# Raw expert weights in four buffers that rotate in program order, one size register, held products flushed earlier, and padding products

## The chip, the cores and the metric

The program runs on one core of one Trainium2 chip, in one launch. The metric is device time in microseconds (us). The kernel before took 292.46 us (median of three runs, 291.24 to 293.19). One further execution was profiled; the rows below are from it.

TensorE (PE) multiplies, with a weight load (PEld) ahead of each product; VectorE (DVE), ScalarE (ACT) and GpSimd (POOL) work element by element; SyncE (SP) issues transfers, and POOL issues the indirect ones (gathers and scatters).

## The reference

Linear attention over four batches, eight heads, 768 positions and 48 channels feeds a gated mixture of eight experts:

```python
for t in range(S):
    cur = einsum('bhd,bhe->bhde', u * k[t], v[t])
    y[t] = einsum('bhd,bhde->bhe', r[t], state + cur)
    state = w[t][..., None] * state + einsum('bhd,bhe->bhde', k[t], v[t])
x = y.transpose(0, 2, 1, 3).reshape(3072, 384)
out = x.copy()
xc = x[x @ w_skip > 0]
logits = xc @ w_gate                 # (tokens, 8)
e_idx = argmax(logits)               # one expert per token
gate = softmax(logits)[e_idx]
for e in range(8):
    m = e_idx == e
    out[those tokens] += gate[m] * (relu(xc[m] @ w1[e]) @ w2[e])   # 384 -> 1024 -> 384
```

Data are float32 throughout, and which expert gets how many tokens is known only at run time.

## The kernel before, in words

**Attention.** The 3072 rows are 24 chunks of 128 positions. A loop over "slots" s runs from -2 to 24, and each slot works on several chunks at once. POOL makes the cumulative products of chunk s+2 (p L370, rk L372, wrk L379, kq L400); DVE makes two scans (L384, L402), rp (L407), two masks (asb L436) and a bonus (psY L448) per slot; PE makes psu L458, the outputs L484 and L490, the scores L420 from rp and kq, the sums L444 and the row products L505. psu, psY, psA0 and psA1 are PSUM banks. SP stores each finished chunk (L520).

**The router.** Tokens are routed in three groups of chunks, (0, 12), (12, 6) and (18, 6). The router is a generator whose steps are dripped into the slots after the group's last chunk, a fixed number per slot (`drip`, `pace`); it makes one-hot rows (`hots`, on DVE or, by `by_act`, ACT) and sums on PE. Pieces for PE that it appends to `held` (the ranks at L562 to L568, the places at L617, into the psu bank) are run by `flush()`, which stands at the end of each slot. A DVE step behind such a piece comes in program order as soon as it has been flushed.

**Expert 0, early.** Slots 22 to 24 and the stretch behind also carry expert 0's first 128 tokens: their indices id0, the gather xg0 (L656), transposes (L671), layer 1 (L151, into psH) and layer 2 (L701, into psO). Then the router's last group gives idr; POOL issues the gather xg1 of expert 0's second 128 tokens (L525) and those of expert 1; the sizes of the experts (`few`, eight digits 0, 1 or 2) go into eight registers of PE (L842); xg1 is transposed (L671) and expert 0's layer 1 follows for them (`second`, L919). For each of four banks it branches: 96 columns where size 0 is positive, 128 else.

**Experts 1 to 7.** Each does layer 1 (L934 to L936) and layer 2 (L958, L964) on up to 256 tokens, with weights split into a high and a low part: the raw weights arrive by SP (`load_weights`, two halves of 1.5 MB for each expert, three transfers each), ACT casts the high part (L131), and POOL or DVE subtract to get the low part (L135). Raw halves lie in buffers r00, r10, r01 and r11. Three more kinds of work fill in: scatters of results (L912), gathers of expert e+2's tokens (L525), and a check of the decay products (wp, L866 to L881).

**What sets the order.** Attention and all engines but SP in the expert phase follow program order. SP's transfers of the expert phase are put in order by a scheduler.

## Time and profile before

| | |
|---|---|
| median of three runs | 292.46 us |
| the profiled execution, whole | 291.64 us |
| its span in the trace | 289.8 us |
| busy share of the span: PE, DVE, POOL, ACT | 91%, 76%, 68%, 52% |
| moved | 65.08 MB, 225 GB/s |

The span is the part of the execution that the trace covers; 1.84 us lie around it. The page lists, for 40 slices of the span, how busy each engine was and which clock PE was granted; the chain of waits follows the work that ended last back to its start; the timeline lists instructions in order of start, with the idle time ahead of each and what ended it.

### The profile page before, as it was taken

How to read it: one execution, taken by the hardware profiler on the slowest of the kernel's cores; microseconds unless marked ns; L12 is line 12 of the kernel's file. 1: busy time of each engine (PE TensorE's matmuls, PEld its weight loads, DVE VectorE, ACT ScalarE, POOL GpSimd, SP SyncE). 2: the span in 40 equal slices, each digit the busy share in tenths (PEclk: the TensorE clock that was granted, in tenths of full speed). 3: DMA queues.
4: the chain of work that ended last, by engine and by line, in shares of the span. 5: the costliest groups of instructions: out<-in, count | busy, mean ns of one | idle time of the engine just before them, and what ended most of it. 6: DMA issues, size and time to landing. Idle time of an engine off the chain costs nothing.

```text
span 289.8 us, 9303 instructions
## 1 busy us (share of the span) xinstructions
PE 263.3 (91%) x3695; PEld 232.8 (80%) x3695; DVE 220.3 (76%) x431; ACT 150.1 (52%) x365; POOL 196.4 (68%) x176
## 2 busy tenths in 40 slices
PE   7769999989899798888986999999999999999990
PEld 2458888878687686677876999997999999998880
DVE  6988999889999879996282355888785788779931
ACT  5134434443467525424530546668694957769710
POOL 6889999999876857769962323783865548545711
PEclk9999999999999899999998699999999999999998
DMA  6999999999978798856097986117678781998001
GB/s 170 241 232 274 276 279 275 270 280 250 276 225 235 220 283 212 263 172 231 29 317 257 349 287 233 55 54 271 250 259 274 253 318 47 323 349 309 29 11 46
DMA packets 27699, 65.08 MB, mean 225 GB/s; under 512 B 4172, under 2 KB 15408, under 8 KB 27638
## 3 DMA queue, kind: packets, MB, share of 16 engines
q1 hardware_dynamic: 25318, 58.39, 66.5%
q0 software_dynamic: 2048, 5.48, 5.5%
q8 instruction: 39, 0.64, 1.0%
q10 hardware_dynamic: 272, 0.39, 0.5%
q14 instruction: 22, 0.18, 0.2%
HBM read 57.20 MB, written 7.86 MB: 225 GB/s over the span
## 4 chain that ended last, share of the span: by engine, by line
PE 69%; DVE 11%; DMA 9%; POOL 4%; issue 3%; ACT 2%; SPq 1%; DVEq 0%; POOLq 0%; ACTq 0%
PE psO L958 17%; PE psH L948 7%; PE psY L484 5%; PE psA L420 5%; PE psH L934 4%; PE psH L936 4%; PE psH L935 4%; DMA wrk<-wrk 4%; PE psX L505 4%; PE psH L151 4%; PE psY L490 4%; PE psY L444 3%; DVE asb L436 3%; PE psO L964 3%; DMA xg<-out,idr 2%
## 5 line engine op out<-in xcount | busy, mean ns | idle before, releaser
L135 POOL TENSOR_TENSOR w2l<-r,w2h 128x512 fp32r<-128x512 f32 x25 | 33.0, 1340 | 15.2 <-ACT w2h L131 14.9
L912 POOL DMA_INDIRECT out<-fin,ids x16 | 20.4, 1275 | 33.5 <-DMA xg<-out,idr 9.5
L400 POOL TENSOR_TENSOR kq<-wrk,q 128x512 f32<-128x512 f32 x24 | 26.9, 1120 | 16.1 <-DVE q L384 10.7
L379 POOL TENSOR_TENSOR wrk<-wrk 128x512 f32<-128x512 f32 x24 | 36.2, 1508 | 1.7
L436 DVE TENSOR_TENSOR asb<-psA,c_sb 128x512 f32<-128x512 f32 x48 | 30.8, 683 | 6.2 <-PE psA L420 5.8
L1001 DVE SCALAR_TENSOR_TENSOR hl<-psH,hh 128x512 fp32r<-128x512 f32 (+1 forms) x32 | 20.8, 654 | 18.5 <-ACT hh L1000 18.5
L958 PE MATMUL psO<-w2h,hh 128*128 128x384 f32 x96 | 32.8, 342 | 0.0
L135 DVE TENSOR_TENSOR w1l<-r,w1h 128x512 fp32r<-128x512 f32 x30 | 32.6, 1102 | 0.0
L958 PE MATMUL psO<-w2l,hh 128*128 128x384 f32 x96 | 32.1, 335 | 0.0
L496 ACT COPY xT<-psY 128x512 f32<-128x512 f32 x24 | 14.1, 586 | 34.0 <-PE psY L490 28.8
L484 PE MATMUL psY<-asb,vN 128*64 128x128 f32 (+1 forms) x384 | 25.8, 276 | 4.9 <-DVE psY L448 4.7
L525 POOL DMA_INDIRECT xg<-out,idr x15 | 17.2, 1145 | 18.6 <-DMA out<-fin,ids 14.0
L131 ACT CAST w2h<-r 128x512 fp32r<-128x512 f32 x48 | 27.5, 648 | 3.4 <-DMA r<-w 3.4
L372 POOL TENSOR_TENSOR rk<-wrk 128x512 f32<-128x512 f32 x22 | 28.1, 1277 | 0.0
L420 PE MATMUL psA<-rp,kq 64*64 64x128 f32 (+1 forms) x768 | 26.5, 256 | 1.1 <-DVE rp L407 0.6
L934 PE MATMUL psH<-xTh,w1h 128*128 128x224 f32 (+1 forms) x96 | 26.8, 279 | 0.0
L936 PE MATMUL psH<-xTh,w1l 128*128 128x224 f32 (+1 forms) x96 | 26.5, 276 | 0.0
L935 PE MATMUL psH<-xTl,w1h 128*128 128x224 f32 (+1 forms) x96 | 26.5, 276 | 0.0
L484 PEld LDWEIGHTS psY<-asb,vN 128*64 128x64 f32 (+1 forms) x384 | 20.4, 130 | 6.5 <-DVE psY L448 6.1
L131 ACT CAST w1h<-r 128x512 fp32r<-128x512 f32 x42 | 25.6, 633 | 0.0
L1000 ACT ACTIVATE hh<-psH 128x512 fp32r<-128x512 f32 (+1 forms) x32 | 18.2, 570 | 12.4 <-PE psH L936 6.7
L420 PEld LDWEIGHTS psA<-rp,kq 64*64 64x64 f32 x768 | 22.6, 136 | 2.3 <-POOL kq L400 0.9
(169 smaller groups left out, 696.3 us busy)
## 6 DMA issues: line engine op xcount, KB each, us to landing
r<-w SPq DMA_DIRECT2D x48, 512.0 KB, 5.3
wrk<-wrk SPq DMA_DIRECT2D x23, 577.9 KB, 6.1
wp<-wrk SPq DMA_DIRECT2D x9, 516.0 KB, 8.0
vN<-vN SPq DMA_DIRECT2D x12, 384.0 KB, 4.8
out<-x SPq DMA_DIRECT2D x24, 192.0 KB, 4.0
vt<-wrk SPq DMA_DIRECT2D x24, 96.0 KB, 5.0
vt<-wrk SPq DMA_DIRECT2D x48, 48.0 KB, 4.4
out<-fin,ids POOLq DMA_INDIRECT x16, 4.4
```

The source lines that it names most:

```text
L131: nc.scalar.copy(hi, raw)
L135: eng.tensor_tensor(lo, raw, hi.bitcast(F32), op=ALU.subtract)
L372: (nc.gpsimd if i > 1 else nc.vector).tensor_tensor(rk.rearrange("p a j -> p (a j)"), t[:, R_OFF:K_OFF], t[:, K_OFF:V_OFF], op=ALU.mult)
L379: nc.gpsimd.tensor_tensor(rk1, rk1, two(1, 1, CW), op=ALU.mult)
L400: nc.gpsimd.tensor_tensor(pairs(kq), pairs(wk["k"]), twice(wk["q"][:, :, 1:HW]), op=ALU.mult)
L420: nc.tensor.matmul(psa[g][j:j + HP, a, j:], wk["kq"][rows, a, j:j + HP], wk["rp"][rows, a, j:], start=True, stop=True)
L436: nc.vector.tensor_tensor(s, psa[g], tri.rearrange("p (o j) -> p o j", o=1).to_broadcast([P, NP, P]), op=ALU.mult)
L484: nc.tensor.matmul(quarter(0, a, g, w), head(i, 2 * a + g, w), wk["asb"][g][:, a], start=False, stop=(c == 0), skip_group_check=True)
L934: nc.tensor.matmul(ps, w1h[:, o:o + P], xh, start=(kc == 0), stop=False)
L935: nc.tensor.matmul(ps, w1h[:, o:o + P], xl, start=False, stop=False)
L936: nc.tensor.matmul(ps, w1l[:, o:o + P], xh, start=False, stop=(kc == KC - 1))
L958: nc.tensor.matmul(pso, h[j, fc][k], w[:, fc * DM:(fc + 1) * DM], start=(i == 0), stop=(i == len(todo) - 1))
```

## The change

Six things change.

1. **Raw buffers.** From expert 2 on, the halves rotate over r11, r01, r00, r10 in this order, each half in one transfer of 1.5 MB where there were three of 512 KB. SP joins the engines in program order. The second half of expert 1 is loaded in slot 23, ahead of the store of chunk 23. Expert 2's halves are made to wait for ACT's copy of the transposed xg1.
2. **Gathers.** xg4 and xg5 (expert 2's tokens) are issued with xg1 to xg3, ahead of the scatters.
3. **Sizes.** DVE multiplies the eight digits by powers of four and sums them; PE loads one register, and each branch tests two bits of it.
4. **Expert 0's second 128 tokens.** The branch goes: always 128 columns. Four memsets on DVE that went with it go too.
5. **Held pieces.** Up to slot 17 `flush()` comes after the scores of the next chunk and ahead of the drip that ends the slot. In the first group ACT makes eight one-hot rows, not six, and DVE four, not six. Two low parts of expert 0's second-layer weights move from slots 21 and 22 to slots 13 and 14 on POOL. In slot 23 the last drip comes after the transposes.
6. **Padding.** In slot 0 PE gets ten products of zeros, 5, 2 and 3 of them, at three places.

```diff
 W_AT = {7: ((0, 1),), 11: ((0, 1),), 15: ((0, 1),), 17: ((0, 0),), 19: ((0, 0),), 20: ((0, 0), (1, 0)),
-        21: ((1, 0), (1, 0))}
+        21: ((1, 0), (1, 0)), 23: ((1, 1), (1, 1), (1, 1))}
 CAST_AT = {9: ((0, 6),), 10: ((0, 7),), 13: ((0, 8),), 14: ((0, 9),), 18: ((0, 10),), 19: ((0, 11),),
            22: ((1, 0), (1, 1)), 23: ((1, 2), (1, 3)), 24: ((1, 4), (1, 5))}
-LOW_AT = {21: ((0, 6), (0, 7), (0, 8)), 22: ((0, 9), (0, 10), (0, 11)), 23: ((1, 0), (1, 1), (1, 2)),
-          24: ((1, 3), (1, 4), (1, 5))}
+LOW_AT = {13: ((0, 6),), 14: ((0, 7),), 21: ((0, 8), (0, 9)), 22: ((0, 10), (0, 11)),
+          23: ((1, 0), (1, 1), (1, 2)), 24: ((1, 3), (1, 4), (1, 5))}
 KEYS_AT = {-2: (), -1: (0,), 0: (1,), 1: (2, 3)}
...
                                                mybir.DependencyReason.DATA),
-                          reason="shared port")
+                          reason="behind the gather")
     WN = ("w1h", "w1l", "w2h", "w2l")
...
     def load_weights(e, q):
-        pool, tag = (wset1[0], "r11") if q and e % 2 and e > 1 else (wset0, ("r00", "r10", "r01")[
-            2 * (e % 2) if not q else 1])
+        pool, tag = (wset0, "r" + ("00", "10", "01", "10")[2 * (e % 2) + q]) if e < 2 else (
+            (wset1[0], "r11"), (wset0, "r01"), (wset0, "r00"), (wset0, "r10"))[2 * (e % 2) + q]
         wr = pool.tile([P, KC * DF], F32, tag=tag, name=f"{tag}_{e}{q}")
         raws[e, q] = wr
-        for i in range(3):
-            o = i * 1024
-            nc.sync.dma_start(wr[:, o:o + 1024],
-                              w12[e, :, q * KC * DF + o:q * KC * DF + o + 1024])
-            yield 1
+        m = 3 if e < 2 else 1
+        w = KC * DF // m
+        for i in range(m):
+            o = i * w
+            yield nc.sync.dma_start(wr[:, o:o + w],
+                                    w12[e, :, q * KC * DF + o:q * KC * DF + o + w])
...
         ohs = keep.tile([P, 1, E], BF16, name="ohs")
+        digit = keep.tile([P, E], F32, name="digit")
         short = keep.tile([1, 1, 1], BF16, name="short")
...
             nc.vector.memset(ohs, 0.0)
+            for e in range(E):
+                nc.gpsimd.memset(digit[FEW - P:FEW - P + 1, e:e + 1], float(4 ** e))
             nc.vector.memset(ex_sb, 1e-9)
...
                                       op=ALU.is_equal)
-            by_act = () if last else range(0, m, 2) if m == MG else (0,)
+            by_act = () if last else [c for c in range(m) if c % 3] if m == MG else (0,)
             order = [c for c in range(m) if c in by_act] + [c for c in range(m) if c not in by_act]
...
                 nc.tensor.transpose(ps[:, kc], xg[j][:, kc * P:(kc + 1) * P], ident)
-            nc.scalar.copy(xT0[j], ps)
-
-        hfs = []
+            copied.append(nc.scalar.copy(xT0[j], ps))
+
+        hfs, copied = [], []
...
             nc.vector.scalar_tensor_tensor(fin0, pso, gate0, xg[0], op0=ALU.mult, op1=ALU.add)
+
+        def pad(k):
+            for _ in range(k):
+                nc.tensor.matmul(psr, warm[:, :P], warm, start=False, stop=True,
+                                 skip_group_check=True)
...
                         later.append(early())
+            if s == 0:
+                pad(5)
             if on(s):
                 update(s)
+            if s == 0:
+                pad(2)
             slot[0], spot[0] = s, 1
...
                 outputs(s)
+            if s == 0:
+                pad(3)
             if s == -1:
...
                     quadratic(s + 1)
+                if s < LATE:
+                    flush()
                 spot[0] = 3
                 drip(2 * pace[0])
-            elif s == n - 1:
-                drip(1)
             for i in KEYS_AT.get(s, (s + 2,)):
...
                     keys(i)
+            if s == n - 1:
+                drip(1)
             if s == n - 2:
...
                 rows_out(s)
-            flush()
+            if s >= LATE:
+                flush()
             for i in LOW_AT.get(s, ()):
...
         idf = keep.tile([P, 2, E], F32, name="idf")
-        few = keep.tile([P, E], I32, name="few")
+        few = keep.tile([P, E], F32, name="few")
+        size_i = keep.tile([P, 1], I32, name="size_i")
         ids = keep.tile([P, 2, E], U32, name="ids")
...
                 done[0] += 1
-        drain(load_weights(1, 1))
         early_low(1)
...
             gather(s, None)
-        step = few[FEW - P:FEW - P + 1]
+        step, sizes = few[FEW - P:FEW - P + 1], size_i[FEW - P:FEW - P + 1]
         nc.vector.tensor_scalar(step, gates[FEW - P:FEW - P + 1, 1], 0.0, None, op0=ALU.is_equal)
...
                                        op0=ALU.is_equal, op1=ALU.add)
+        nc.vector.tensor_tensor(step, step, digit[FEW - P:FEW - P + 1], op=ALU.mult)
+        with nc.allow_low_precision(reason="whole numbers"):
+            nc.vector.tensor_reduce(sizes, step, axis=AX, op=ALU.add)
         for k in range(done[0], 6 * FC - 4):
             next(todo)
-        regs = nc.values_load_multi_w_load_instructions(
-            step, engines=[mybir.EngineType.PE], min_val=0, max_val=2)[1]
-        size = dict(enumerate(regs))
+        size = nc.values_load_multi_w_load_instructions(
+            sizes, engines=[mybir.EngineType.PE], min_val=0, max_val=2 * (4 ** E - 1) // 3)[1][0]
         early_tokens(1)
...
                                      accum_out=viol[:, i:i + 1])
-                if e == E - 1:
-                    fetch_w()
...
-        def second(bank, q, m):
-            for i in range(2):
-                for kc in range(KC):
-                    hidden(bank[:, 0, i * P:i * P + m], xT0[1][:, :, :m], 2 * q + i, kc)
-
         def layer1(e, q, bank):
...
             def larger():
-                with tc.If(size[e] > 0) as cmp:
+                with tc.If((size & 4 ** e) > 0) as cmp:
                     rounded(MID)
...
                 return
-            with tc.If(size[e] > 1) as cmp:
+            with tc.If((size & 2 * 4 ** e) > 0) as cmp:
                 for ps, kc, o in tiles:
...
             h, hf = {}, {}
-            if e == 0:
-                for bank in psh:
-                    nc.vector.memset(
-                        bank[:, 0].rearrange("p (i j) -> p i j", i=2)[:, :, MID - P:], 0.0)
             for q in range(FC // 2):
...
                 if e == 0:
-                    with tc.If(size[0] > 0) as cmp:
-                        second(bank, q, MID - P)
-                    with cmp.Else():
-                        second(bank, q, P)
+                    for i in range(2):
+                        for kc in range(KC):
+                            hidden(bank[:, 0, i * P:(i + 1) * P], xT0[1], 2 * q + i, kc)
                 else:
...
                 flag_sums()
-            if e < E - 2:
-                drain(load_weights(e + 2, 0))
+            if e == 0 or 1 < e < E - 2:
+                drain(load_weights(max(e + 2, 3), 0))
             if e + 1 < E:
...
                 scatter(0, fin0)
-            if e + 2 < E:
+            if 0 < e < E - 2:
                 for s in (2 * e + 4, 2 * e + 5):
...
                         check_w(e, 1 if e < E - 1 else E)
+                        if W_FROM - 1 <= e < E - 1:
+                            fetch_w()
+                            fetch_w()
                 pso = psos[j]
...
                     psx = ps1.tile([P, 512], F32, tag="psT", name=f"psX3{e}", bufs=2)[:, :DM]
-                    with tc.If(size[e] > 1) as cmp:
+                    with tc.If((size & 2 * 4 ** e) > 0) as cmp:
                         layer2_few(e, hf, pso, psx)
...
             more(12, left=0)
-            if e + 2 < E:
-                drain(load_weights(e + 2, 1))
-            if W_FROM - 1 <= e < E - 1:
-                fetch_w()
-                fetch_w()
+            if e == 0 or 1 < e < E - 2:
+                drain(load_weights(max(e + 2, 3), 1))
         with tc.manual_schedule(engines={nc.tensor.engine, nc.scalar.engine, nc.vector.engine,
-                                         nc.gpsimd.engine}):
+                                         nc.gpsimd.engine, nc.sync.engine}):
+            for s in (4, 5):
+                gather(s, moe)
+            for q in range(2):
+                for load in load_weights(2, q):
+                    beside(load, copied[1])
             nc.gpsimd.memset(zero, 0.0)
```

How the instructions move shows in four places. On SP, at the end of attention (x22 and x23 are the rows of the last two chunks, r10_11 the raw second half of expert 1; in names like r11_20 the first pair of digits is the buffer, the second the expert and its half), before:

```order
L520 DMA out<-x22_2574 128x384
L520 DMA out<-x23_2619 128x384
L111 DMA r10_11_2743<-w12 128x1024 x3
L111 DMA r01_30_3129<-w12 128x1024 x3
L987 UNCONDITIONAL_BRANCH x2
L111 DMA r11_31_3233<-w12 128x1024 x2
```

and with the change:

```order
L524 DMA out<-x22_2597 128x384
L113 DMA r10_11_2641<-w12 128x1024 x3
L524 DMA out<-x23_2646 128x384
L113 DMA r11_20_2849<-w12 128x3072
L113 DMA r01_21_2851<-w12 128x3072
L113 DMA r00_30_2905<-w12 128x3072
L113 DMA r10_31_2959<-w12 128x3072
```

Expert 1's half moves ahead of the last store, and what followed it is now expert 2's two halves, which wait for the copy of xg1's transposes.

On PE, at the hand-over from expert 0's early layer 2 (psO0) to its second 128 tokens (psX01 are their transposes, psH0 the first bank of layer 1), before:

```order
L842 TENSOR_LOAD few_2632
L842 ISA x16
L671 MATMUL psX01_2844<-c_sb_98,xg1_65 128x128 x3
L701 MATMUL psO0_2713<-w2h0_0_1134,h0l_100 128x384 x4
L987 COMPARE_AND_BRANCH
L151 MATMUL psH0_2868<-xT01_69,r00_00_2056 128x96 x6
L987 UNCONDITIONAL_BRANCH
L151 MATMUL psH0_2868<-xT01_69,r00_00_2056 128x128 x6
L987 UNCONDITIONAL_BRANCH
```

and with the change:

```order
L863 TENSOR_LOAD size_i_2660
L863 ISA x2
L675 MATMUL psX01_2807<-c_sb_98,xg1_65 128x128 x3
L705 MATMUL psO0_2741<-w2h0_0_1153,h0l_100 128x384 x4
L152 MATMUL psH0_2831<-xT01_69,r00_00_2052 128x128 x6
L152 MATMUL psH1_2832<-xT01_69,r00_00_2052 128x128 x6
```

The register set-up shrinks from sixteen instructions to two, and the branches between the banks are gone.

On DVE, in slot 13 (oh0 and rnk0 are the first group's chosen experts and ranks, pr0 is PE's sum of ranks, q15 the next chunk's scan), before:

```order
L276 TENSOR_TENSOR oh0_1481<-key_124,pss_127 128x96
L276 COPY pss_127<-c_sb_98 128x12x2
L276 TENSOR_TENSOR rnk0_1534<-pr0_1502,oh0_1481 128x96
L384 SCALAR_TENSOR_TENSOR q15_1536<-p15_1435,pss_127 128x260
L397 RECIPROCAL p15_1435<-q15_1536 128x4
```

and with the change:

```order
L278 TENSOR_TENSOR oh0_1501<-key_125,pss_128 128x96
L278 COPY pss_128<-c_sb_98 128x12x2
L388 SCALAR_TENSOR_TENSOR q15_1539<-p15_1454,pss_128 128x260
L401 RECIPROCAL p15_1454<-q15_1539 128x4
L406 SCALAR_TENSOR_TENSOR pss_128<-p15_1454,pss_128 128x260
L471 TENSOR_TENSOR psu_116<-psu_116,q14_1440 128x4x48
L411 TENSOR_TENSOR rp15_1570<-wrk0_85,pss_128 128x512
L440 TENSOR_TENSOR asb0_14_1589<-psA0_118,c_sb_98 128x512
L440 TENSOR_TENSOR asb1_14_1591<-psA1_119,c_sb_98 128x512
L452 TENSOR_TENSOR psY_117<-psY_117,vt2_90 128x2x256
L278 TENSOR_TENSOR rnk0_1616<-pr0_1602,oh0_1501 128x96
```

The rank product, which waits for PE's sum, moves behind the slot's whole attention work.

On POOL, ahead of slot 22's end (kq23 is the last chunk's key product, xg0 the gather for expert 0's first tokens, w2l0 the low parts), before:

```order
L379 TENSOR_TENSOR wrk2_87<-wrk2_87 128x2x256
L656 DMA xg0_64<-out,id0_70 128x384
L400 TENSOR_TENSOR kq23_2438<-wrk2_87,q23_2419 128x512
L135 TENSOR_TENSOR w2l0_0_1135<-r10_01_1028,w2h0_0_1134 128x512 x6
```

and with the change:

```order
L383 TENSOR_TENSOR wrk2_87<-wrk2_87 128x2x256
L404 TENSOR_TENSOR kq23_2460<-wrk2_87,q23_2441 128x512
L660 DMA xg0_64<-out,id0_70 128x384
L136 TENSOR_TENSOR w2l0_0_1154<-r10_01_1047,w2h0_0_1153 128x512 x4
```

The gather changes places with kq23, and two of the six low parts behind it are gone from here.

## Rows read from the trace of the kernel before

**Rows 1.** Windows of attention and experts: busy PE, PEld, DVE, ACT, POOL; PEclk, DMA share, GB/s.

```profile
80.00:100.00 20.00, 16.99 (x401) 14.88 (x405) 18.92 (x48) 12.52 (x33) 14.64 (x14) 0.98 0.79 227
180.00:200.00 20.00, 20.00 (x130) 19.75 (x130) 16.45 (x23) 14.98 (x35) 13.50 (x11) 1.00 0.32 103
```

**Rows 2.** Chain of waits at the hand-over: start, length, what.

```profile
149.58 6.46 DMA xg<-out,idr
```

**Rows 3.** Windows of 1 us (columns as in the first group).

```profile
100.00:101.00 1.00, 1.00 (x32) 1.00 (x26) 0.65 (x2) 0.44 (x1) 1.00 (x3) 0.50 0.89 206
154.00:155.00 1.00, 0.00 (x0) 0.00 (x0) 0.00 (x0) 0.00 (x0) 0.14 (x1) 1.00 0.99 406
158.00:159.00 1.00, 1.00 (x7) 1.00 (x6) 0.24 (x3) 0.00 (x0) 0.00 (x0) 0.50 0.60 115
180.00:181.00 1.00, 1.00 (x8) 1.00 (x7) 0.77 (x2) 1.00 (x4) 0.12 (x1) 1.00 0.00 0
```

**Rows 4.** Timeline of PE at the hand-over: start, length, what, [idle ahead, releaser].

```profile
153.12 0.87 PE L701 MATMUL psO<-w2h,h0l 128*128 128x384 f32 x4
156.18 0.52 PE L671 MATMUL psX<-c_sb,xg 128*128 128x128 f32 x3 [2.18 <-DMA xg<-out,idr]
157.27 8.85 PE L151 MATMUL psH<-xT,r 128*128 128x96 f32 x48
165.95 0.82 PE L903 MATMUL psX<-c_sb,xg 128*128 128x128 f32 x6
```

**Rows 5.** PE's sequencer at line 842: count, ns min/median/max, first and last start.

```profile
L842 PEldq FUSED_REGOPS  x8: 146/146/160, 153.5 to 155.6; - x8
L842 PEldq TENSOR_LOAD <-few x1: 792/792/792, 152.6 to 152.6; - x1
```

**Rows 6.** Gathered tiles xg, from issue to landing.

```profile
DMA to landing us min/median/max: 3.2/6.4/7.8
```

**Rows 7.** Timeline of PE, expert 0's early layer 1.

```profile
141.58 0.94 PE L151 MATMUL psH<-xT,r 128*128 128x128 f32 x6
143.31 2.27 PE L151 MATMUL psH<-xT,r 128*128 128x128 f32 x18
```

**Rows 8.** Timeline of DVE, slots 13 to 17 and two late slots.

```profile
81.04 0.26 DVE L276 TENSOR_TENSOR rnk<-pr,oh 128x96 f32<-128x96 f32 x1 [0.43 <-PE pr L568]
88.89 0.74 DVE L276 TENSOR_TENSOR hot<-iota,pss 128x256 bf16<-128x256 bf16 x2
102.25 1.29 DVE L436 TENSOR_TENSOR asb<-psA,c_sb 128x512 f32<-128x512 f32 x2 [1.61 <-PE psA L420]
105.28 0.27 DVE L454 MEMSET psu<- 128x256 f32 x1 [1.14 <-PE psu L617]
128.39 0.69 DVE L448 TENSOR_TENSOR psY<-psY,vt 128x512 f32<-128x512 f32 x1
133.03 0.69 DVE L448 TENSOR_TENSOR psY<-psY,vt 128x512 f32<-128x512 f32 x1
```

**Rows 9.** Timeline of PE in slot 16.

```profile
98.32 1.11 PE L484 MATMUL psY<-asb,vN 128*64 128x128 f32 x16 [1.86 <-DVE psY L448]
```

**Rows 10.** Timeline of POOL around the gather xg0.

```profile
130.35 1.23 POOL L656 DMA_INDIRECT xg<-out,id  x1 [0.18 <-issue]
131.61 1.14 POOL L400 TENSOR_TENSOR kq<-wrk,q 128x512 f32<-128x512 f32 x1
132.69 7.41 POOL L135 TENSOR_TENSOR w2l<-r,w2h 128x512 fp32r<-128x512 f32 x6
```

**Rows 11.** The page's DMA issues: that gather, median us to landing.

```profile
xg<-out,id POOLq DMA_INDIRECT x1, 7.2
```

**Rows 12.** Timeline of PE: the first use of that gather.

```profile
137.69 0.52 PE L671 MATMUL psX<-c_sb,xg 128*128 128x128 f32 x3
```

**Rows 13.** Timeline of PE, start-up and slot 0.

```profile
6.57 3.02 PE L709 MATMUL psw<-warm 128*128 128x512 bf16 x12
18.90 0.67 PE L444 MATMUL psY<-rk,ubk_sb 64*64 64x128 f32 x16 [1.81 <-ACT xT L496]
```

## The prediction

> **What bounds the kernel now.** I began with windows of 20 us. In attention DVE is busy 18.92 of 20 us and PE 16.99; in the expert phase PE is busy 20.00 of 20, at full granted clock [rows 1]. So an attention edit pays if it takes work or waits from DVE, and an expert edit pays only where PE stands or is slowed. Next I read the chain of waits at the seam between the two: its largest single piece there is not an engine but the gather xg1, 6.46 us from issue to landing [rows 2]. Then the 1-us windows there: while the gather is under way no engine but POOL does anything, and the DMA engines are full (share 0.99, 406 GB/s); two microseconds later PE works again, but at a granted clock of 0.50, its lower level of 1.2 GHz [rows 3]. The timeline shows what PE did: the last product of early layer 2 ends at 153.99 (153.12 + 0.87), it idles 2.18 us, and expert 1's transposes start at 165.95 [rows 4]. That hand-over of 11.96 us is the largest place where PE is either idle or slow after attention.
>
> **Hand-over: the register.** Before, PE's sequencer loads the sizes at 152.6 (0.79 us) and decodes eight registers from 153.5 to 155.76, about 0.3 us each [rows 5]. Had the gather been quick, this alone would have held PE until 155.8. After, one register is decoded, but DVE does two more tiny operations first. I price them at 0.35 us together: the rank product and the memset, both of larger shapes, are busy 0.26 and 0.27 us, and such pairs overlap [rows 8]. So PE may go on at 152.6 + 0.35 + 0.79 + 0.3 = 154.05.
>
> **Hand-over: the gather.** Before, its 6.46 us run against raw weights that SP issues around it, six transfers of 512 KB next to each other in its order. Gathers range from 3.2 to 7.8 us with a median of 6.4 [rows 6]; the 3.2 is one whose flight falls in a stretch where the DMA engines idle (180 to 181: share 0.00) [rows 3]. After, expert 1's half is loaded before the last store, and expert 2's halves are tied to ACT's copy of xg1, so they cannot start before it lands. What still shares the engines is the last store and four more gathers, each issued 1 us or so behind. I take 3.4 us, near the quiet end: issued at 149.58, it lands at 153.0, ahead of the register. The other end is the old 6.46.
>
> By the Trainium skill (DMA: Bandwidth & Descriptors, Queues, rings and completion order) a DMA engine takes turns between the queue rows that have work, a packet at a time, so a gather on POOL's queue would share with SP's loads and not stand behind them. By it, taking the loads away would buy little; the 3.2 against 6.46 speaks for more, but no row here isolates it, so the rule's outcome is rival B.
>
> **Hand-over: the products.** Before, 48 records of 96 columns span 157.27 to 166.12, most of them at the lower clock [rows 3, 4]. After, they have 128 columns. At full clock the early ones of that size give (2.27 − 0.94) / 12 = 0.111 us a record [rows 7], so 48 take 5.33 us. The clock fell behind the idle 2.18 us; after, PE idles some 0.1 us (153.99 to 154.05 and a little) and I expect no fall. So: transposes at 154.15, products 1.09 us later as before (156.18 to 157.27) at 155.24, expert 1 at 160.6. **Gain 165.95 − 160.6 = 5.35 us.** The four branches between banks and DVE's four memsets go at nothing: PE's records there are seamless. At the bad end (gather as late as before, lower clock all along) the products take 48 × 0.222 = 10.66 against 8.68 between their start and expert 1's: a loss of 2.0.
>
> **Attention: DVE.** Three waits of DVE on router pieces stand in slots 13 to 18: 0.43 us for the ranks, 1.61 for scores that come late, 1.14 for the places [rows 8]. The first goes, since the rank product now comes behind the slot's own work. The second comes from PE being late and slow: it idled 1.86 us for a late bonus, and its clock fell to 0.50 behind that [rows 3, 9]; the bonus was late because DVE had made hot rows in front of it. The third goes because the places are flushed half a slot earlier, and DVE finds them done. Two of six hot rows go to ACT, 0.74 / 2 × 2 = 0.74 us less the overlap of about 0.08, so 0.66 [rows 8]; ACT is busy 12.5 of 20 us [rows 1] and hides them. Sum 0.43 + 1.61 + 1.14 + 0.66 = **3.84 us**. The low end for this sum is 1.1 (only ranks and hot rows); I take the whole, because DVE is the engine that is full there [rows 1].
>
> **Attention: POOL.** Two low parts of 1.24 us each (7.41 / 6) [rows 10] move to slots 13 and 14. They delay the next kq by about 0.7 us. PE waits there for DVE, not for kq, so I cost them at nothing; if that cover is gone, 2 × 1.24 = 2.5 us. They leave POOL's queue behind kq23, where nothing is late.
>
> **Attention: the gather xg0.** It lands 7.2 us after its issue at 130.35 [rows 10, 11], at 137.55, and PE uses it at 137.69 [rows 12]: no slack. Now kq23 (1.14 us) stands ahead of it [rows 10], and its indices come a slot's part later. PE can do other work of the slot only up to the transposes. The lower end is 0, the upper 1.8: kq's 1.14 and one bonus of 0.69 [rows 8] ahead of the index sums. I take **0.9 lost**, since the kq that goes first also lets the scores start 1.2 us earlier.
>
> **The rest at nothing.** One transfer of 1.5 MB in place of three: the casts then wait for all of it, but expert 2's halves now have buffers of their own and start at 155, where before they stood in SP's queue behind expert 3's; PE's 20.00 of 20 [rows 1] is the bound. The added register arithmetic at each branch runs on a sequencer ahead of the products. SP in program order puts x23's store behind r10_11, which waits for POOL's last low part from its buffer; in the time before that would be 131.6 + 1.14, less overlap, + 1.23 for the gather + 4 × 1.24 = about 138.8 [rows 10], with PE still some microseconds from x23's rows, so SP is free when they come. Ten padding products at 3.02 / 12 = 0.25 us at most are 2.5 us; a single idle behind them is 1.81 [rows 13] and absorbs all but 0.7. That is the upper end; I take nothing, since the last three of the ten are put right ahead of that idle. A gain there I exclude: the clock in slot 0 is at its upper level in the page's slices.
>
> **Sum.** Against the profiled execution of 291.64: 291.64 − 5.35 − 3.84 + 0.9 = 283.35, say **283.4 us**. The median of the runs shown is 0.82 above the profiled one; I make no shift for that.
>
> **Rivals.**
> - **A. Attention keeps its waits.** PE still idles near 1.9 us in slots 15 or 16, the clock falls there [rows 9], and the 1.61 + 1.14 stay with DVE. For it: DVE's load per slot falls by only 0.66 over four slots. Against it: the rank wait that began the shift is gone. 283.4 + 2.75 = 286.1.
> - **B. The gather lands as late as before**, four further gathers and the store taking the loads' place. Then PE idles 2 us, the clock falls, and the hand-over changes by 0 to +2.0: 291.64 − 3.84 + 0.9 = 288.7, and with up to 2.0 more 290.7; middle 289.7. Against it: the 3.2 [rows 6]. The Trainium skill's rule on turns between rows points this way for the loads.
> - **C. Slower: xg0 comes a slot too late.** Its indices are the result of a router step, and PE's slot order can't step over the transposes at 137.69 [rows 12]. If the step slips past DVE's turn in the slot, xg0 is late by a slot, 133.03 − 128.39 = 4.64 us [rows 8]; PE idles over twice the 2.18 that was enough for a fall of the clock [rows 3, 4], and with its waits in the two slots left the clock stays low for about half of the 16.3 us of work up to 153.99, which costs 8.2 more. 283.4 + 4.64 + 8.2 = 296.2. It decides once lateness and clock together pass 8.3, the forecast's whole gain.
> - **D. The hand-over's gain is given back.** PE comes to expert 1 five microseconds sooner, and finds its casts or low parts late, which PE's own lateness hid: 288.7. For it: DVE subtracts low parts there beside its other work and is busy 16.45 of 20 us [rows 1]. Against it: PE is never idle in experts before, and expert 1's second half is loaded earlier than it was.
>
> **How the numbers follow.** Chances: forecast 0.62, A 0.17, B 0.09, C 0.05, D 0.07. The forecast's own range is 281 (no loss at xg0, gather and register a little quicker: −0.9, −0.5, −1) to 285 (xg0 at 1.8, attention's sum a unit short). The range reaches over A and towards B: 281 to 288. What differs by less than 1%, 2.9 us from 292.46, can't be told from no change here: below 289.5 counts as faster. Forecast, A, most of D and a part of B would lie there by their middles; I give the forecast and A 0.78 of their 0.79 and half of B and D 0.06: 0.84. Within 1%: the other half of B and D, and forecast and A missed, 0.11. Slower: C, 0.05.
>
> **What would show it.** In the profile after: the gather xg1 at 3 to 4 us, PE's idle at the hand-over below 0.5 us, granted clock 1.00 all through 128-column products of 5.3 us in all; one decode in place of eight. DVE's waits of 0.43, 1.61 and 1.14 gone, and no fall of the clock in slots 15 to 17. The transposes of xg0 within 2 us of the end of the sums ahead of them. The forecast is wrong if the gather takes 6 us without loads beside it, if the clock falls without an idle stretch, or if PE shows gaps at casts in experts 1 and 2.

## The result, and the profile after

The changed kernel takes **284.36 us** (median of six runs, 283.48 to 288.64) where the kernel before takes 292.75 (six runs, 290.75 to 294.59). The ratio, 0.9706 with a 95% interval of 0.9649 to 0.9763, leaves out two of the six runs, 287.75 and 288.64, that fell in a slower state. The profiled execution took 284.55 us, span 282.6, against 291.64 and 289.8: 7.1 us less, where 8.3 were forecast.

The hand-over on PE's timeline after (start, length, what; a bracket would name an idle ahead, which one of 0.03 us doesn't get); it answers to [rows 4]:

```profile
150.25 0.86 PE L705 MATMUL psO<-w2h,h0l 128*128 128x384 f32 x4
151.14 0.52 PE L675 MATMUL psX<-c_sb,xg 128*128 128x128 f32 x3
152.23 5.63 PE L152 MATMUL psH<-xT,r 128*128 128x128 f32 x48
157.69 0.71 PE L921 MATMUL psX<-c_sb,xg 128*128 128x128 f32 x5
```

PE now idles 0.03 us, from 151.11 to 151.14, and expert 1's transposes start 6.58 us after the last early product ahead of xg1's transposes, not 11.96 (four more early products stand behind those transposes, before and after). What it waited for, first the register (PE's sequencer, ns min/median/max, start), answering to [rows 5]; then the gathers xg issued from 146.5 to 152.9 (the DMA view: count, median us to landing), to [rows 2, 6]:

```profile
L863 PEldq TENSOR_LOAD <-size_i x1: 487/487/487, 150.1 to 150.1; - x1
L863 PEldq FUSED_REGOPS  x1: 170/170/170, 150.7 to 150.7; - x1
```

```profile
xg<-out,idr POOLq DMA_INDIRECT x3, 3.4
```

The register is ready at 150.87, 0.24 us before PE comes free, and the gather, issued at 146.84, is down 3.4 us later, where it took 6.46. That is close for the register: in every profile of the changed kind (the changed kernel and the eleven experiments on it) in which the gather is not the last to come, PE goes on some 0.3 us after the last register is decoded, and in seven of them PE idles 0.38 to 0.46 us for it. The windows of 1 us (busy PE, PEld, DVE, ACT, POOL; PEclk, DMA share, GB/s) show why, and that the clock stays up, against [rows 3]:

```profile
149.00:150.00 1.00, 1.00 (x8) 1.00 (x7) 0.85 (x6) 0.00 (x0) 0.69 (x2) 1.00 0.32 105
153.00:154.00 1.00, 1.00 (x11) 1.00 (x10) 0.01 (x1) 0.08 (x1) 0.87 (x1) 1.00 1.18 209
```

In attention, the clearest change is the early gather xg0, against [rows 10 to 12]: POOL's timeline, its landing in the DMA view of 128 to 134, and PE's use of it:

```profile
127.79 1.12 POOL L404 TENSOR_TENSOR kq<-wrk,q 128x512 f32<-128x512 f32 x1 [2.30 <-DVE q L388]
129.08 1.23 POOL L660 DMA_INDIRECT xg<-out,id  x1 [0.18 <-DMA r<-w]
```

```profile
xg<-out,id POOLq DMA_INDIRECT x1, 3.3
```

```profile
134.91 0.55 PE L675 MATMUL psX<-c_sb,xg 128*128 128x128 f32 x3
```

It lands at 132.4, 2.5 us before PE wants it. Before, it landed just in time.

To place the time, each profile is cut at DVE's bonus psY of chunks 13 and 23, at the hand-over, and at PE's last product. The two ends after, on DVE's timeline (a stretch ends where the instruction ends, start plus length):

```profile
80.01 0.69 DVE L452 TENSOR_TENSOR psY<-psY,vt 128x512 f32<-128x512 f32 x1
135.10 0.70 DVE L452 TENSOR_TENSOR psY<-psY,vt 128x512 f32<-128x512 f32 x1 [1.76 <-ACT sblk L480]
```

| stretch, us | before | after | change | forecast |
|---|---|---|---|---|
| start to the bonus of chunk 13 | 79.73 | 80.70 | +0.97 | 0 |
| bonus of chunk 13 to chunk 23 | 58.70 | 55.10 | −3.60 | −3.84 + 0.9 |
| on to the last early product ahead of xg1's transposes | 15.56 | 15.31 | −0.25 | 0 |
| hand-over | 11.96 | 6.58 | −5.38 | −5.35 |
| expert 1 to PE's last product | 117.30 | 117.28 | −0.02 | 0 |
| on to the end of the span | 6.55 | 7.63 | +1.08 | 0 |

The sum is −7.2, the change of the span.

### The profile page after: what moved, and what is told of

Read it like the earlier page. It is cut to its first block, busy times and chain, and to the rows that moved or that the text cites. A ratio compares the mean times of both kernels' runs of the same rounds, so it can differ in the third digit from the quotient of the medians.

```text
span 282.6 us, 9308 instructions
## 1 busy us (share of the span) xinstructions
PE 258.8 (92%) x3704; PEld 227.8 (81%) x3705; DVE 215.4 (76%) x427; ACT 151.7 (54%) x369; POOL 195.2 (69%) x184
## 4 chain that ended last, share of the span: by engine, by line
PE 62%; DMA 15%; DVE 13%; issue 3%; POOL 2%; ACT 1%; SPq 1%; DVEq 0%; POOLq 0%; ACTq 0%
PE psO L971 18%; PE psH L961 7%; DMA vt<-wrk 6%; PE psH L947 4%; PE psY L488 4%; PE psH L948 4%; PE psH L949 4%; DVE asb L440 4%; PE psH L152 3%; PE psA L424 3%; DMA vN<-vN 3%; PE psO L977 3%; DVE psY L452 3%; PE psX L509 3%; DMA wrk<-wrk 2%
## 5 line engine op out<-in xcount | busy, mean ns | idle before, releaser
L930 POOL DMA_INDIRECT out<-fin,ids x16 | 18.5, 1157 | 36.9 <-DVE w2l L136 13.7
L136 POOL TENSOR_TENSOR w2l<-r,w2h 128x512 fp32r<-128x512 f32 x25 | 34.7, 1404 | 7.5 <-ACT w2h L132 7.2
L529 POOL DMA_INDIRECT xg<-out,idr x15 | 15.9, 1062 | 18.8 <-DMA out<-fin,ids 11.6
L424 PE MATMUL psA<-rp,kq 64*64 64x128 f32 (+1 forms) x768 | 25.7, 251 | 1.5 <-ACT ubk_sb L319 1.5
L136 DVE TENSOR_TENSOR w1l<-r,w1h 128x512 fp32r<-128x512 f32 x30 | 25.5, 865 | 0.0
L424 PEld LDWEIGHTS psA<-rp,kq 64*64 64x64 f32 x768 | 21.7, 133 | 3.0 <-POOL kq L404 2.0
```

The lines of the kernel that those rows point to most:

```text
L136: eng.tensor_tensor(lo, raw, hi.bitcast(F32), op=ALU.subtract)
L424: nc.tensor.matmul(psa[g][j:j + HP, a, j:], wk["kq"][rows, a, j:j + HP], wk["rp"][rows, a, j:], start=True, stop=True)
```

## The experiments

Runs of one version differ by 1 to 7 us, and the median of the kernel before, run anew beside each group of experiments, lay there between 294.0 and 295.5, so the stretches of the profiles decide, and the whole time only where it is clear. Ratios are to the kernel before in the same group. The other changed versions without a fall of the clock up to there reach the bonus of chunk 13 between 79.1 and 81.4 us, so the +0.97 of the first line is within what one program does. The clean value of chunk 13 to 23 (no fall of the clock in it) repeats to 0.1: 55.10 after, and 55.22, 55.22, 55.20, 55.18 and 55.11 in the experiments on the loads, the branch, the store, the low parts and the copies. The expert stretch repeats less well than the table's 117.30 and 117.28 suggest: in the twelve profiles of the changed kind it takes 117.3 to 118.7.

**What the gather meets.** First without the wait that ties expert 2's halves to the gather:

```diff
-                for load in load_weights(2, q):
-                    beside(load, copied[1])
+                for load in load_weights(2, q):
+                    pass
```

> The changed kernel, but the two halves of expert 2 no longer wait for the copy of the transposed xg1: SP issues them as soon as their buffers are free. Theory (raw weights in flight stretch the gather): xg1 takes 5 to 6.5 us in place of 3.39, PE idles 1 to 2 us longer at the hand-over, perhaps at the lower clock behind it, hand-over 8 to 12 us in place of 6.58, the whole 1.5 to 6 us longer. Rival (the gather takes turns with the loads and is hardly stretched): xg1 at most 4.2 us, hand-over within 0.5 of 6.58, the whole the same.

Measured: 285.68 us, 0.9694 of before (0.963 to 0.9758), hand-over 6.95. It doesn't tell the theories apart: SP's timeline shows that the loads start late anyway, at 153.39, behind the transposes at 152.14. SP's last wait ahead of them is 1.5 us for the last products of early layer 2 (PE, L705), and it is the same wait with the tie.

```profile
137.99 1.36 SPq L113 DMA_DIRECT2D r<-w  x3
141.85 0.34 SPq L524 DMA_DIRECT2D out<-x  x1
153.39 5.83 SPq L113 DMA_DIRECT2D r<-w  x3
```

So it is that wait, presumably for memory that the chosen buffers take over, that keeps expert 2's halves out of the way; the tie adds nothing. Next, expert 1's half behind the store of chunk 23 (it goes from the table of slot 23 to just ahead of `early_low(1)`):

```diff
-        21: ((1, 0), (1, 0)), 23: ((1, 1), (1, 1), (1, 1))}
+        21: ((1, 0), (1, 0))}
...
+        drain(load_weights(1, 1))
         early_low(1)
```

> The changed kernel, but the second half of expert 1 is loaded behind the store of chunk 23, as before; expert 2's halves still wait for the copy. Theory (only what flies during the gather counts): the three transfers start near 142 and are nearly down at 146.8 when the gather starts; xg1 3.4 to 4.5 us, hand-over 6.6 to 7.7, the whole up to 1 us longer. Rival (loading that half early is what brings the gain): xg1 over 5 us, or PE idle at the casts of expert 1, the whole 2 us longer or more.

Measured: 285.83 us, 0.970 (0.965 to 0.9751), hand-over 6.95. The half's transfers keep the DMA engines busy (shares of 0.80 to 0.99) until 146, the gather is issued at 145.36, and PE's idle of 0.40 is ended by the register and not by the gather, whose landing this profile does not give. So, as the theory had it, a half that is nearly down when the gather starts does not hold PE up. The test of contention itself is the same half tied to the sum that precedes the gather, so that 1.5 MB fly beside it (it leaves the table here too):

```diff
+                marks.append(vec.last)
                 gather(1, None)
...
+        for load in load_weights(1, 1):
+            beside(load, marks[0])
         early_low(1)
```

> The changed kernel, but the three transfers of expert 1's second half, 1.5 MB, wait for the sum that gives idr, so that they start together with the gather xg1. Theory (raw weights in flight stretch the gather): xg1 takes 5 us or more in place of 3.39, PE idles 1 to 2.5 us, hand-over 8 to 9.5 us in place of 6.6 to 6.95. Rival (the gather takes turns with the loads): xg1 at most 4.2 us, hand-over under 7.5.

Measured: 287.78 us, 0.9804 (0.973 to 0.9878). The chain of waits and PE's timeline:

```profile
148.75 6.10 DMA xg<-out,idr
```

```profile
152.16 0.86 PE L706 MATMUL psO<-w2h,h0l 128*128 128x384 f32 x4
154.99 0.52 PE L676 MATMUL psX<-c_sb,xg 128*128 128x128 f32 x3 [1.97 <-DMA xg<-out,idr]
156.07 5.62 PE L152 MATMUL psH<-xT,r 128*128 128x128 f32 x48
161.54 0.71 PE L924 MATMUL psX<-c_sb,xg 128*128 128x128 f32 x5
```

The gather takes 6.10 us, PE idles 1.97, and the hand-over is 8.51: raw weights in flight do stretch the gather. This was shown by putting them back. Of the 4.7 us by which this execution's span exceeds the changed kernel's, 1.93 are the hand-over; the rest lies elsewhere (PE stood 2.02 us at 115.5 for nothing that the profile shows, the clock fell at 127), so the whole time is no measure of the gather. The Trainium skill (DMA: Bandwidth & Descriptors, Queues, rings and completion order) says that queue rows take turns by the packet; sharing of that kind fits, but it does not make the gather cheap: beside 1.5 MB it takes 6.10 in place of 3.4.

**The registers.** Eight again, in the changed kernel (DVE's two operations and the tests of bits go with it):

```diff
-        size = nc.values_load_multi_w_load_instructions(
-            sizes, engines=[mybir.EngineType.PE], min_val=0, max_val=2 * (4 ** E - 1) // 3)[1][0]
+        regs = nc.values_load_multi_w_load_instructions(
+            step, engines=[mybir.EngineType.PE], min_val=0, max_val=2)[1]
+        size = dict(enumerate(regs))
```

> The changed kernel with eight size registers of PE again, as before; loads still behind the gather, no branch in expert 0. Theory (the registers are a second wait behind the gather's): the last register is ready about 152.8 in the time of the changed kernel (load at 149.8, 0.5 to 0.8 us, eight of 0.3), PE idles about 1.7 us, hand-over 8.3 us in place of 6.58 if the clock stays, up to 11 if it falls as behind the idle 2.18; the whole 1.7 to 4.5 us longer. Rival (the gather alone bound the hand-over): hand-over 6.6, the whole the same.

Measured: 289.23 us, 0.9796 (0.9745 to 0.9847). The sequencer and PE:

```profile
L860 PEldq FUSED_REGOPS  x8: 146/146/160, 153.2 to 155.2; - x8
L860 PEldq TENSOR_LOAD <-few x1: 780/780/780, 152.3 to 152.3; - x1
```

```profile
155.58 0.52 PE L675 MATMUL psX<-c_sb,xg 128*128 128x128 f32 x3 [2.34 <-issue]
156.67 5.62 PE L152 MATMUL psH<-xT,r 128*128 128x128 f32 x48
```

PE idles 2.34 us, and the profile names no DMA as its end: the gather was issued at 148.97, 6.6 us before PE goes on at 155.58, and the last register is decoded at 155.4. The hand-over is 8.89. The other half of the pair, one register in the kernel before (the same edit the other way, with DVE's two operations):

> The kernel before with the sizes in one register of PE, all else as it was. Theory (two waits stood side by side at the hand-over, and the gather among the raw weights is the other one): the gather xg1 takes 6 to 6.5 us as before, PE idles about 2.0 us in place of 2.18, hand-over 8.8 us if the clock stays up and near 12 if it falls; the whole the same as before within 1%. Rival (the registers were the wait): PE idles under 0.5 us, the whole 2 us shorter or more.

Measured: 293.24 us, 0.994 (0.989 to 0.9991). Gather 6.18, PE idle 1.90, hand-over 9.89:

```profile
158.30 0.85 PE L674 MATMUL psX<-c_sb,xg 128*128 128x128 f32 x3 [1.90 <-DMA xg<-out,idr]
158.80 1.63 PE L704 MATMUL psO<-w2h,h0l 128*128 128x384 f32 x4
160.22 6.23 PE L151 MATMUL psH<-xT,r 128*128 128x96 f32 x48
```

So two waits of like length stood side by side. Either one alone keeps some 2 us of idle; only both together take it away. (Both hand-overs are still 2 to 3 us shorter than the 11.96, since the clock stayed up in one and fell for a shorter time in the other.)

**The columns.** The branch to 96 or 128 columns back, with its memsets:

```diff
-                    for i in range(2):
-                        for kc in range(KC):
-                            hidden(bank[:, 0, i * P:(i + 1) * P], xT0[1], 2 * q + i, kc)
+                    with tc.If((size & 3) > 0) as cmp:
+                        second(bank, q, MID - P)
+                    with cmp.Else():
+                        second(bank, q, P)
```

> The changed kernel with the branches to 96 or 128 columns in expert 0's second tokens, and DVE's four memsets, as before; one register. Theory (at full clock a record takes time by its columns, and the branches are hidden): 48 records of 0.083 in place of 0.115 us, hand-over about 5.2 in place of 6.58, the whole 1.3 us shorter. Rival one (a record has a floor, so fewer columns buy nothing): hand-over 6.6. Rival two (each branch holds the products up by 0.2 us or more): hand-over 6 to 7.5, no gain or a loss.

Measured: 287.1 us, 0.9739 (0.9682 to 0.9795), hand-over 6.65. PE's products, and the weight loads of the same stretch, with 96 columns:

```profile
152.12 5.60 PE L152 MATMUL psH<-xT,r 128*128 128x96 f32 x48
```

```profile
L152 PEld LDWEIGHTS psH<-xT,r 128*128 128x128 f32 x48 | 5.4, 192 | 0.2 <-ACT xT L676 0.2
```

5.60 us with 96 columns, 5.63 with 128: at the upper clock the columns are free here. Their 48 weight loads are busy 5.4 us whichever it is, so it is likely that they set the pace; no run varies them. The branches cost nothing that shows (hand-over 6.65 against 6.58), and buy nothing.

**The flush.** All held pieces at the slot's end:

```diff
-                if s < LATE:
-                    flush()
...
-            if s >= LATE:
-                flush()
+            flush()
```

> The changed kernel with all held pieces flushed at the slot's end, as before. Theory (the early flush took away DVE's waits for the ranks and the places): both waits return, 0.4 and 1.1 us, the router's steps come a slot earlier again; from the masks of chunk 13 to those of chunk 23 58 us in place of 55.1, the whole 1.5 to 3 us longer. Rival (the attention gain came from the one-hot rows and from chance in the clock): within 0.5 us of 55.1 on that stretch, the whole the same.

Measured: 287.52 us, 0.9844 (0.9696 to 0.9992); chunk 13 to 23 56.60 us with no fall of the clock in it, 1.5 more than clean. The wait for the ranks is back on DVE, the one for the places is not; and the router's second group, a slot earlier again, sends the gather xg0 among two transfers of raw weights (DMA view, 128 to 137):

```profile
82.44 0.26 DVE L278 TENSOR_TENSOR rnk<-pr,oh 128x96 f32<-128x96 f32 x1 [0.43 <-PE pr L572]
```

```profile
r<-w SPq DMA_DIRECT2D x2, 512.0 KB, 6.9
out<-x SPq DMA_DIRECT2D x2, 192.0 KB
xg<-out,id POOLq DMA_INDIRECT x1, 7.2
```

0.7 of the 1.5 stands before chunk 21 and 0.8 behind. What the 0.8 is the trace does not name.

**The one-hot rows.** Six of the first group on ACT, as before:

```diff
-            by_act = () if last else [c for c in range(m) if c % 3] if m == MG else (0,)
+            by_act = () if last else range(0, m, 2) if m == MG else (0,)
```

> The changed kernel with six of the first group's one-hot rows on DVE and six on ACT, as before. Theory (DVE bounds slots 13 to 17): from the masks of chunk 13 to those of chunk 17 0.66 us more than 22.1, that is 22.8, and the whole 0.7 longer, less than a run's spread. Rival (another engine bounds those slots): 22.1 still. Second rival (more work on DVE makes PE idle long enough for its clock to fall): 25 or more.

Measured: 288.19 us, 0.9869 (0.9739 to 0.9998). Chunk 13 to 17 takes 22.60 against 22.12: 0.48, near the 0.66. Chunk 13 to 23 is 58.08, but a fall of the clock lies in it (122 to 126), so the rest of the 3 us can't be put down to the rows.

**The low parts.** Both back in slots 21 and 22:

```diff
-LOW_AT = {13: ((0, 6),), 14: ((0, 7),), 21: ((0, 8), (0, 9)), 22: ((0, 10), (0, 11)),
+LOW_AT = {21: ((0, 6), (0, 7), (0, 8)), 22: ((0, 9), (0, 10), (0, 11)),
```

> The changed kernel with the two low parts back in slots 21 and 22 on POOL, behind kq23 and the gather xg0. Theory (POOL has room in both places): chunks 13 to 15 0 to 0.3 us quicker, POOL's low parts end about 145 in place of 142.7, still ahead of the gather xg1; the store of chunk 23, behind expert 1's half in SP's queue, goes out up to 1 us later; the whole within 0.5 us. Rival (the late low parts hold the raw buffer, the half, the store behind it and so the gather): xg1 issued 1 to 2 us later against the last masks, hand-over 1 to 2 us longer.

Measured: 285.66 us, 0.9769 (0.9565 to 0.9972), chunk 13 to 23 55.18, hand-over 6.94. POOL has room in both places; the move is worth nothing.

**The padding.** Without the ten products (the three calls of `pad` in slot 0 left out):

> The changed kernel without the ten padding products of slot 0. Theory (they lie in PE's idle time): masks of chunk 3 done within 0.3 us of the changed kernel's 32.4 or, where they cost a little, up to 0.7 earlier; clock and total the same. Rival one (they caused the loss of 1.04 us that the changed kernel shows up to chunk 3 against before): 31.4. Rival two (they keep PE's clock up in the slots that follow): a granted clock of 0.5 somewhere before 40 us, and 1 us or more longer.

Measured: 287.16 us, 0.9792 (0.9616 to 0.9968). The bonus of chunk 3 is done at 31.93, where versions with pads and no fall of the clock ahead of it have it between 31.5 and 32.4: neither rival. The clock fell to half in slot 0 in four of the ten profiles of changed versions with pads, and not in this one nor in the next experiment; in the kernel before with one register, which has no pads, it did fall there. The pads don't keep the clock up.

**Two tries at a better kernel.** Slot 0 without pads and with ACT's two copies of the output weights behind its copy of the outputs:

```diff
-                nc.scalar.copy(wgo_sb[:, :, E + 1:], wgp_sb[:, 1::2, :2 * D])
-                nc.scalar.copy(wgo_sb[:, :, :E + 1], wgp_sb[:, 1::2, 2 * D:])
...
+            if s == 0:
+                nc.scalar.copy(wgo_sb[:, :, E + 1:], wgp_sb[:, 1::2, :2 * D])
+                nc.scalar.copy(wgo_sb[:, :, :E + 1], wgp_sb[:, 1::2, 2 * D:])
             if on(s):
                 rows_out(s)
```

> The changed kernel without the ten padding products, and with ACT's two copies of the output weights in slot 0 moved from the slot's top to just ahead of the row products of chunk 0, so that ACT's copy of chunk 0's outputs no longer waits for their load. Theory (that wait, which ends PE's idle 2.50 us in slot 0, is what makes the start late and lets the clock fall there): PE idles under 1 us in slot 0, masks of chunk 3 done at 30.5 to 31.3 us in place of 32.4 (32 without pads), no fall of the clock before 40 us, the whole 1 to 2 us shorter than the changed kernel. Rival (chunk loads bound the first slots, POOL waits for them 0.6 and 1.6 us): 31.9 or more, the whole the same.

Measured: 286.4 us, 0.9762 (0.9698 to 0.9826). PE's idle of 2.50 in slot 0 is gone, but chunk 3 is done at 31.71, inside the 31.5 to 32.4 of the versions above and 0.22 before the version without pads. POOL still waits there for a chunk's load, which speaks for the rival but doesn't prove it:

```profile
20.36 0.62 POOL L374 TENSOR_TENSOR p<-wrk 128x260 f32<-128x260 f32 x1 [1.06 <-DMA wrk<-wrk]
```

And three one-hot rows of the second group on ACT:

```diff
-            by_act = () if last else [c for c in range(m) if c % 3] if m == MG else (0,)
+            by_act = () if last else [c for c in range(m) if c % 3] if m == MG else (0, 1, 2)
...
-            if rare:
-                rare.pop(0)()
+            for _ in range(len(rare) if s >= LATE else min(1, len(rare))):
+                rare.pop(0)()
... (the same at the slot's other place for rare)
```

> The changed kernel with three one-hot rows of the second group on ACT in place of one, all run at their next place in the slot (three there in place of one). Theory (the slot between the masks of chunks 20 and 21, 8.2 us, is DVE's: two rows of 0.33 us fewer shorten it, and nothing behind is late): 7.5 us there, masks of chunk 13 to chunk 23 54.5 in place of 55.1 to 55.2, gather xg0 still about 3.3 us and early, the whole 0.7 shorter, about 284 where the changed kernel takes 284.4 to 285.8. Rival (ACT's rows delay its copies for PE, or the places wait for ACT): 8.2 or more, the whole the same or up to 1 us longer.

Measured: 287.56 us, 0.9775 (0.9719 to 0.9831). Chunk 20 to 21 takes 7.61 in place of 8.21, as the theory had it, but PE waits for the rows:

```profile
124.86 0.19 PE L621 MATMUL psu<-sg,hot 128*128 128x40 bf16 x1 [0.54 <-ACT hot L605]
125.94 0.42 PE L621 MATMUL psu<-sg,hot 128*128 128x40 bf16 x10 [0.89 <-ACT hot L605]
```

The clock fell at 127 in this profile, so the rest of its attention can't be compared. Nothing here beats the changed kernel.

## Why the prediction was right, point by point

- **Hand-over, forecast −5.35, measured −5.38.** Each part held: gather 3.4 us, register ready ahead of PE, PE's idle 0.03, products at the upper clock in 5.63 against 5.33. That it fits to 0.03 is luck: in nine other profiles of the changed kind, those in which neither wait was put back, the hand-over is 6.6 to 7.0. It is 2.15 us of idle and 3.2 us of clock. The 2.15 is shown by putting back either wait (1.97 and 2.34 of idle). The 3.2 is less certain than I made it: I took the fall of the clock for the consequence of an idle 2.18. Behind idles of 2.34 and 1.97 in the changed program the clock stayed at 1.00, and behind 1.90 in the kernel before with one register it fell to half. In the twelve profiles of the changed kind the clock never fell at the hand-over, in the two of the other it fell both times; what decides is open. The branches and their 96 columns are not it: in that last kernel the clock fell in the transposes ahead of them, as its 1-us windows show:

```profile
157.00:158.00 1.00, 0.00 (x0) 0.00 (x0) 0.00 (x0) 0.00 (x0) 0.00 (x0) 1.00 0.97 374
158.00:159.00 1.00, 0.70 (x4) 0.73 (x5) 0.00 (x0) 0.00 (x0) 0.00 (x0) 0.67 0.24 89
```

- **The bad end of +2.0** rested on 128 columns costing more than 96. At the upper clock they don't (5.63 against 5.60); at the lower no run has 128 columns.
- **Attention on DVE, forecast −3.84, measured −3.60 between chunks 13 and 23.** The size is right, its parts only in part. The wait of 0.43 for the ranks returns with the late flush, the one of 1.14 for the places does not, and the one-hot rows are 0.48 of the forecast 0.66. The 1.61 was PE late behind a fall of the clock [rows 3, 9]. I said that fewer rows ahead of it would take away the idle that let it fall. After, PE idles 1.61 there, and the clock holds:

```profile
98.12 1.09 PE L488 MATMUL psY<-asb,vN 128*64 128x128 f32 x16 [1.61 <-DVE psY L452]
```

  The kernel before with one register, whose attention is that of the kernel before, shows how much was clock (its own fall, at 84, lies three slots earlier). PE's idle there is the same 1.86, the clock holds behind it, and DVE's wait for the scores is 0.28 in place of 1.61, while the wait for the places is still there:

```profile
102.00 1.09 PE L487 MATMUL psY<-asb,vN 128*64 128x128 f32 x16 [1.86 <-DVE psY L451]
104.61 1.29 DVE L439 TENSOR_TENSOR asb<-psA,c_sb 128x512 f32<-128x512 f32 x2 [0.28 <-PE psA L423]
107.42 0.27 DVE L457 MEMSET psu<- 128x256 f32 x1 [0.92 <-PE psu L620]
```

  So of the 1.61 some 1.3 came with the clock of that execution, and 0.9 of the 1.14 did not. Which edit took the places' wait away no run shows: it stays away with the late flush and with six one-hot rows on DVE.
- **The clock as a whole.** The hand-over's 3.2 and this 1.3 make 4.5 of the 7.2 us. That is not the luck of one profile: the mean granted clock is 0.975 over 41 executions of the kernel before that stand beside the experiments (0.958 to 0.989), and 0.990 over the six of the changed kernel (0.983 to 0.994). So a higher clock comes with the change. By which part of it is open: no single step put back took it down again (0.983 to 0.990 as the mean of each experiment on the changed kernel), and one register in the kernel before has 0.977.
- **The gather xg0, forecast +0.9: the step that failed.** I gave it its old 7.2 us and a later issue. Issued a slot's part later in the order, it no longer meets the two transfers of raw weights that SP sends in that slot: these go out 4.3 us ahead of it (124.75 and 129.08), where before it was 0.36 (129.99 and 130.35). It takes 3.3, and lands 2.5 us early. The cost is nothing; the late flush, which puts it among the transfers again, has 7.2 back. I had seen this effect at xg1 and not looked for it here.
- **What I didn't list:** the end of the program, +1.08. From PE's last product to the end of the span it is 6.5 us in both profiles of the kernel before's kind, and 7.1 to 7.9 in all twelve of the changed kind. The last scatter lands alike (3.3 and 3.4 us); the rest lies in the engines' last step behind it, and its cause is open. With the +0.97 of the start and against the 0.9 of xg0 it makes most of the 1.1 us by which the forecast was too low.
- **Rivals.** A's idle was there (1.61 in slot 16), and DVE's wait for the scores went because the clock held behind it, so that A failed partly by luck; B fell with the 3.4, C with xg0's early landing, D with 117.28 against 117.30 us of experts. Pads and low parts at nothing, as forecast; the single transfers of 1.5 MB no run takes back.

## What to carry to other kernels

Where two waits of the same length end at the same place, taking one away leaves the idle of the other (1.90 and 2.34 us here, of 2.18); cost them as a pair. The small gathers on the critical path took 3.3 to 3.4 us without bulk loads beside them and 6.1 to 7.2 with, so look at what every queue sends in the microseconds around its issue, and move the bulk or the gather. A gain that rests on the granted clock should be counted apart from the one that rests on idle time, since single falls come and go between executions of one kernel; the mean clock over many executions tells whether a change moves it.

## What the runs showed that I had not expected

The clock's falls are not tied to one place or one length of idle. They came in slot 0, about 84 us, in slot 16, behind the masks of chunk 21 (at 126 to 127 us, with six one-hot rows at 122.8), or at the hand-over; versions that do the same there had one or none. In the eight-register version it fell behind an idle of 1.35 us (below, PE's timeline and the window) and not behind its 2.34:

```profile
127.22 1.97 PE L488 MATMUL psY<-asb,vN 128*64 128x128 f32 x16 [1.35 <-DVE psY L452]
```

```profile
128.00:129.00 1.00, 1.00 (x12) 0.78 (x8) 0.93 (x3) 0.00 (x0) 0.58 (x1) 0.50 0.91 295
```

The changed kernel idles 1.34 at the same place, and its clock stays at 1.00. In eleven of the twelve profiles of the changed kind PE idles 1.34 or 1.35 us there, and behind it the clock fell in four: with eight registers, without pads, with six one-hot rows, and with the half beside the gather. One such fall costs about 1.4 us between chunks 13 and 23 where nothing else differs (56.53 and 56.61 against 55.1 to 55.2). The Trainium skill (TensorE: Matmul & The Clock Gate, Part 1) says of a kernel's start that the same kernel shows a different number of slow products from run to run. These profiles show the like in the middle of a kernel, at the same idle in nearly the same program.
